# Transforms of a fused FFT and mixture-of-experts kernel: each scatter of 128 token rows waits for a PSUM copy of its own

## The chip, the cores and the metric

The kernel runs on one core of one Trainium2 chip. The metric is the time of the whole program in device microseconds (us), and lower is better. Names of engines are those of the profile: PE is the matrix engine, DVE the vector engine, ACT the scalar engine, POOL is GpSimd, SP the queue that issues most DMAs. L164 means line 164 of the kernel before.

## What is computed

The input x has 8 batches of 3072 rows with 256 values each, in fp32. The program computes the real part of a 2-D Fourier transform of each batch, sends every resulting row (a token, 24576 in all) to one of 8 experts, and runs a second network over all tokens:

```python
X = np.fft.fft(np.fft.fft(x, axis=1), axis=2).real          # 8 x 3072 x 256
x = X.reshape(24576, 256)
e = argmax of the cosine of x with the 8 expert rows; gate = its softmax probability
x = gate * (np.maximum(x @ w1[e], 0) @ w2[e])                # per token, its own expert
out = ((x @ w_a) * (x @ w_b)) @ w_out
```

## The kernel before, in words

The program has three stages one after the other. The **transforms** (span up to about 558 us) take the 8 batches in turn. The **experts** follow (up to about 1790 us), and then the second network. Only the transforms are touched.

The work of a batch b has two halves.

- `s1(b, s)`, 8 steps. Each step has two groups (h = 0, 1) of four matmuls at L343 into one of two PSUM banks, and behind each group ACT copies the bank to `yt` (L347). A profile shows each of these fp32 matmuls as two records, so that a whole half has 128 of them.
- `s2(b, t)` with `s3(b, t - 2)`, 12 steps. A step multiplies `yt` into two PSUM tiles `psb` and `psa` (L360, 8 records), ACT copies `psb` to `zs` (L361), DVE makes `zc` (L363), and two steps later PE multiplies both into a third tile (L376, L379), which ACT copies to `qs` (L387) and DVE adds and subtracts into the token rows `xo` (L388, L390). There are two buffers for each of these PSUM tiles, and one `xo` buffer for even and one for odd batches, so the rows of batch b must have left `xo` before step t = 2 of batch b + 2 writes there.

When the rows of a batch are complete, `route` (DVE, a generator that goes on by a few instructions at each step) computes for each row its place `posi` among the rows of its expert. `spread` (L164) then sends 128 rows of `xo` to these places in DRAM (the tensor `xs`) by an indirect DMA that POOL issues: the **scatter**. A batch has 24 of them, the transforms issue 168, and the rest of the 192 for `xs` fall in the first expert groups. POOL also computes two of the four `fold_v` pieces of the next batch's input (L244).

The order on each engine is written out by hand: work that has no step of its own is appended to lists (`act_q`, `dve_q`, `pool_q`) and taken off by `drain(queue, n)` at fixed places. Before the change `pool_q` holds both the folds and the scatters. It is drained by 2 in each step of s1 and by 3 in each step of s2. As `route` of batch b - 1 delivers its 24 places about four steps into s2 of batch b, POOL gets them in a row there, and issues them one behind the other: a burst. A scatter waits for the scatter eight before it and for its rows, for nothing else.

At the end of the transforms what is left of the 168 is issued. The expert stage begins with group 0; for group 1 POOL multiplies rows by their gates (`weigh`, L737, L738) and computes a low part (`halves`, L755), and the weight splits on ACT and DVE (L727, L728) write memory that the even `xo` buffer held, so they wait for its scatters to land.

Of the kernel before, what the change touches and what calls it, by code (L numbers as in the profile page):

```python
# [34 lines left out]
NROWS = E * REGION + GT  # L35
# [102 lines left out]
def moe_kernel(ctx, tc, x, emb, tau, w1, w2, wa, wb, wo, pa, pt, pr, nat, out):  # L138
    nc = tc.nc
    ve, sc, gp, pe, sy = nc.vector, nc.scalar, nc.gpsimd, nc.tensor, nc.sync  # L140
    dep = mybir.DependencyInfo(mybir.DependencyClass.Sync, mybir.DependencyReason.DATA)

    dram = ctx.enter_context(tc.tile_pool(name="dram", bufs=1, space=DRAM))
    xs = dram.tile([NROWS, ROW], F32, name="xs")
# [16 lines left out]
    scatters = []  # L161

    def spread(idx_ap, src, dst, last, key):
        i = gp.indirect_dma_start(  # L164
            out=dst[:, :],
            out_offset=bass.IndirectOffsetOnAxis(ap=idx_ap, axis=0),
            in_=src,
            in_offset=None,
            bounds_check=last,
            oob_is_err=False,  # L170
        ).ins
        tc.declare_no_dep(i, group=key, reason="rows of different tokens")
        tc.add_to_no_dep_group(key, i)
        return i


    p1 = ExitStack()
    p1b = ExitStack()
# [33 lines left out]
    def bank():  # L212
        uses[0] += 1
        return banks[uses[0] % 2][:, 0:384]
# [8 lines left out]
    def load_x(n):  # L223
        b, c = divmod(n, 4)
        if b == B:
            return
        t = xr_p.tile([96, 8, D], F32, name="xr")
        sy.dma_start(t, x[b].rearrange("(p n) d -> p n d", p=96)[:, 8 * c:8 * c + 8, :])
        xr[b, c] = t

    def pair(b, c):
        if (b, c) not in xf:
            xf[b, c] = big[(4 * b + c) % 6][0:96, :].rearrange("p (n d) -> p n d", n=8)
        return xr[b, c], xf[b, c]

    def fold_u(b, c, h):
        a, f = pair(b, c)
        n = slice(4 * h, 4 * h + 4)
        ve.tensor_tensor(f[:, n, 1:128], a[:, n, 1:128], a[:, n, 255:128:-1], ALU.add)

    def fold_v(b, c, eng, h):
        a, f = pair(b, c)
        n = slice(4 * h, 4 * h + 4) if h is not None else slice(0, 8)
        eng.tensor_tensor(f[:, n, 129:256], a[:, n, 1:128], a[:, n, 255:128:-1], ALU.subtract)  # L244

    def fold_e(b, c):
        a, f = xr.pop((b, c)), xf[b, c]
        sc.copy(f[:, :, 0:256:128], a[:, :, 0:256:128])
# [86 lines left out]
    def s1(b, s):  # L335
        f = xf[b, s // 2]
        state["step"] += 1
        if s == 0:
            yts[b] = [yt_p.tile([128, NQ, 128], F32, name=f"yt{h}") for h in range(2)]
        for h in range(2):  # L340
            ps = bank()
            for n in range(4):
                pe.matmul(ps[:, 96 * n:96 * n + 96], lhsT=f[:, 4 * (s % 2) + n, 128 * h:128 * h + 128],  # L343
                          rhs=f1[0:96, :], start=True, stop=True)
            dst = yts[b][h][:, :, 16 * s:16 * s + 16].rearrange("p q (n c) -> p q n c", c=4)
            src = ps.rearrange("p (n q c) -> p q n c", n=4, c=4)
            sc.copy(dst, src)  # L347
            if b:
                drain(act_q, 1)

    def s2(b, t):
        state["step"] += 1
        ya, yb = yts[b]
        za = z_p.tile([128, 2, 137], F32, name="zc")
        zb = z_p.tile([128, 2, 137], F32, name="zs")
        pb = psb.tile([128, 2, 138], F32, name="psb")
        pa_ = psa.tile([128, 512], F32, name="psa")[:, 0:274].rearrange("p (i m) -> p i m", i=2)
        for p, y, r in ((pb, yb, rhb), (pa_, ya, rha))[::1 if t else -1]:
            for i in range(2):
                pe.matmul(p[:, i, :], lhsT=y[:, 2 * t + i, :], rhs=r, start=True, stop=True)  # L360
        sc.copy(zb, pb[:, :, 0:137])  # L361
        for i in range(2):
            ve.scalar_tensor_tensor(za[:, i, :], sgnx, pb[:, i, 137:138], pa_[:, i, :], ALU.mult, ALU.add)  # L363
            advance()
        zt[b, t] = (za, zb)
# [41 lines left out]
        if t1 == NT:  # L407
            act_q.append(lambda: square(b, 1, 11))

    act_q, dve_q, pool_q, routes = [], [], [], []  # L410

    def drain(q, n):
        for _ in range(min(n, len(q))):
            q.pop(0)()

    def folds(b):
        for c in range(4):
            dve_q.append(lambda c=c: fold_u(b, c, 0))
            dve_q.append(lambda c=c: fold_u(b, c, 1))
            if c < 2:  # L420
                pool_q.append(lambda c=c: fold_v(b, c, gp, None))
            else:
                dve_q.append(lambda c=c: fold_v(b, c, ve, 0))
                dve_q.append(lambda c=c: fold_v(b, c, ve, 1))

            def rest(c=c):
                fold_e(b, c)
                load_x(4 * b + c + 3)

            dve_q.append(lambda c=c, rest=rest: act_q.insert(0, rest))  # L430

    seg = {}
    for n in sorted({2 * (t1 - t0) for c in CHUNKS.values() for t0, t1 in c} | {2 * NT}):
        s = c1.tile([128, E, n], F32, name=f"seg{n}")
# [15 lines left out]
    def route(b, t0, t1, turn):  # L450
# [16 lines left out]
        for q in range(2):  # L467
            yq = y[:, q, :].rearrange("p (t one) -> p t one", one=1)
            for i, n_ in enumerate((3, 3, 2)):
                c = MAIN + LGC[i]  # L470
# [68 lines left out]
        for i in range(h):  # L539
            for q in range(2):  # L540
                pool_q.append(lambda a=posi[:, q * h + i:q * h + i + 1], r=xo[b][:, NT * q + t0 + i, 0:ROW]:
                              scatters.append(spread(a, r, xs, NROWS - 1, "xs")))
        yield
        if b == HB - 1 and t1 == NT:
            yield from table1(new)
# [3 lines left out]
    def advance(n=1):  # L549
        for _ in range(n):  # L550
            if routes:
                for g in list(routes):
                    r = next(g, 0)
                    if r == 0:
                        routes.remove(g)
                    if r != 1:
                        break

    def start_route(b, t0, t1):
        routes.append(route(b, t0, t1, state["next"]))  # L560
        state["next"] += 1
# [361 lines left out]
    def first(c):  # L923
        for h in range(2):
            fold_u(0, c, h)
        fold_v(0, c, gp if c != 2 else ve, None)

    for b in range(B):
        last = b == B - 1
        if not last:  # L930
            folds(b + 1)
        for s in range(8):
            if b == 0 and s < 6:
                if s == 0:
                    routes.append(embed())
                if s % 2 == 0:
                    first(s // 2 + 1)
                else:
                    fold_e(0, s // 2 + 1)
                    load_x(s // 2 + 4)  # L940
            s1(b, s)
            drain(pool_q, 2 if b or s > 5 else 0)
            if b == 0:
                advance(7)
                drain(dve_q, s > 3)
                continue
            if s == 0:
                s3(b - 1, 10)
                s3(b - 1, 11)
                post(b - 1, 9, 12)  # L950
                act_q.append(lambda b=b - 1, c=CHUNKS.get(b - 1, ((0, NT),))[-1]: start_route(b, *c))
            if last:
                drain(act_q, s < 3)
                advance(8)
                if s == 0:
                    assert "tab1" in half
                    load_w(0)
                if s == 4:
                    load_w(1)
                if s in (4, 5):  # L960
                    split_w(0, s - 4)
            elif s < 3:
                drain(dve_q, 3 if s else 2)
                drain(act_q, s)
            else:
                advance(7)
        if b == 0:
            while routes:
                advance()
            su.close()  # L970
        chunks = {t1 + 1: (t0, t1) for t0, t1 in CHUNKS.get(b, ())}
        if last:
            for g in range(2):
                load_g(g)
        for t in range(NT + (2 if last else 0)):
            if t < NT:
                s2(b, t)
            if t >= 2:
                s3(b, t - 2)
            if t in (5, 8, 11):  # L980
                post(b, t - 5, t - 2)
            if t == NT + 1:
                break
            if t - 1 in chunks:
                act_q.append(lambda b=b, c=chunks[t - 1]: start_route(b, *c))
            if t % 3:
                drain(dve_q, 1)
            drain(act_q, 2)
            drain(pool_q, 3)
            if last:  # L990
                advance(1)
                if t == 6:
                    weigh(0)
                if t == 8:
                    turn(0)
        drain(dve_q, 20)
    drain(pool_q, (B - 1) * 2 * NT - len(scatters))
    assert len(scatters) >= (B - 1) * 2 * NT
    p1b.close()
# [294 lines left out]
```

## Time and profile before

| | before |
|---|---|
| median of 3 runs | 4059.99 us (4057.02 to 4069.61) |
| profiled execution, its own time | 4083.66 us |
| profiled execution, span | 4081.7 us |
| busy share of the span: PE, PE weight loads, DVE, ACT, POOL | 95%, 86%, 76%, 42%, 28% |
| mean granted TensorE clock | 0.956 of full speed |

The span runs from the first to the last instruction. The profile page shows the whole program; the change concerns only the first seventh of it, so its shares say little here. The slices of the page, tables of busy time by stretch, and instructions in order of time within one batch are what to read.

### The profile page before, as it was taken

The page shows a single profiled execution, that of the slowest core. Times are in us where ns is not written, and L with a number is a line of the kernel's source. Part 1 is how long each engine was busy: PE and PEld are TensorE (multiplying, and loading weights), DVE is VectorE, ACT ScalarE, POOL GpSimd, SP SyncE. Part 2 cuts the span into 40 slices and gives each one's busy share as a digit, 9 for nine tenths or more (in the row PEclk, how much of TensorE's full clock was granted, in tenths as well). Part 3 has the DMA queues.
Part 4 walks back from the last instruction along what each step waited for, and adds up shares of the span by engine and source line. Part 5 has one row for each costly group of instructions (what it writes and reads, how often), then busy time and mean ns, then how long its engine had stood idle before and what let it go on. Part 6 is the DMA issues. An engine that isn't in the chain of part 4 may idle for free.

```text
span 4081.7 us, 67996 instructions
## 1 busy us (share of the span) xinstructions
PE 3859.6 (95%) x25556; PEld 3515.0 (86%) x25556; DVE 3084.0 (76%) x5097; ACT 1698.2 (42%) x3025; POOL 1123.4 (28%) x1017
## 2 busy tenths in 40 slices
PE   8675789999999999999999999999999999999998
PEld 8574789999999999988888888888888888888887
DVE  6343378888888888777877778787877778777876
ACT  4233355666666666643333333333333333333332
POOL 2425245666666665300000000011000000000001
PEclk8577589999999999999999999999999999999999
DMA  5223225533233323133334334444433333443331
GB/s 146 86 84 104 90 65 161 179 117 111 77 108 113 117 75 98 48 122 135 137 136 148 138 139 138 138 144 144 138 136 137 135 138 137 149 138 138 138 128 66
DMA packets 255046, 497.83 MB, mean 122 GB/s; under 512 B 151540, under 2 KB 184060, under 8 KB 245884
## 3 DMA queue, kind: packets, MB, share of 16 engines
q1 hardware_dynamic: 236284, 442.04, 33.4%
q0 software_dynamic: 18432, 51.44, 3.5%
q8 instruction: 201, 3.29, 0.3%
q14 instruction: 129, 1.06, 0.1%
HBM read 568.14 MB, written 95.14 MB: 163 GB/s over the span
## 4 chain that ended last, share of the span: by engine, by line
issue 56%; PE 22%; POOL 9%; DVE 6%; another core or an unknown queue 3%; ACT 2%; DMA 1%; SPq 0%; POOLq 0%; ACTq 0%; DVEq 0%
PE ps L343 4%; POOL out_dram L164 4%; PE psh L772 3%; PE psh L773 2%; PE psh L771 2%; DVE s L728 2%; POOL xl L755 2%; PE psy L793 2%; PE psy L794 2%; PE psy L795 2%; PE psb L360 1%; PE psa L360 1%; ACT s L727 1%; PE ps L376 1%
## 5 line engine op out<-in xcount | busy, mean ns | idle before, releaser
L164 POOL DMA_INDIRECT out_dram<-o,ig x192 | 214.1, 1115 | 2095.1 <-ACT o L1189 2043.6
L1185 PE MATMUL po<-wo,gl 128*128 128x256 f32 x2304 | 652.0, 283 | 19.2 <-DVE gl L1167 19.2
L1162 ACT CAST gh<-big 128x512 fp32r<-128x512 f32 x576 | 358.0, 621 | 743.6 <-DVE big L1156 743.6
L1183 PE MATMUL po<-wo,gh 128*128 128x256 f32 x2304 | 647.9, 281 | 0.5 <-ACT gh L1162 0.5
L1184 PE MATMUL po<-wo,gh 128*128 128x256 f32 x2304 | 645.7, 280 | 0.0
L1115 PE MATMUL pp<-xo,slab 128*128 128x512 f32 x1440 | 580.3, 403 | 8.2 <-DVE big L1141 6.8
L728 DVE TENSOR_TENSOR s<-big,s 128x1024 fp32r<-128x1024 f32 x412 | 535.4, 1300 | 55.0 <-ACT s L727 54.3
L1117 PE MATMUL pp<-xo,slab 128*128 128x512 f32 x1440 | 569.7, 396 | 0.0
L1116 PE MATMUL pp<-xo,slab 128*128 128x512 f32 x1440 | 566.6, 393 | 0.0
L1184 PEld LDWEIGHTS po<-wo,gh 128*128 128x128 f32 x2304 | 434.1, 188 | 89.9
L1183 PEld LDWEIGHTS po<-wo,gh 128*128 128x128 f32 x2304 | 432.5, 188 | 88.5 <-ACT gh L1162 0.9
L772 PE MATMUL psh<-xl,s 128*128 128x256 f32 x1648 | 471.6, 286 | 20.6 <-POOL xl L755 17.8
L793 PE MATMUL psy<-hh,s 128*128 128x256 f32 x1648 | 466.9, 283 | 0.0
L794 PE MATMUL psy<-hl,s 128*128 128x256 f32 x1648 | 466.4, 283 | 0.0
L795 PE MATMUL psy<-hh,s 128*128 128x256 f32 x1648 | 465.9, 283 | 0.0
L771 PE MATMUL psh<-xh,s 128*128 128x256 f32 x1648 | 464.5, 282 | 1.4 <-ACT xh L754 1.4
L773 PE MATMUL psh<-xh,s 128*128 128x256 f32 x1648 | 464.7, 282 | 0.0
L1185 PEld LDWEIGHTS po<-wo,gl 128*128 128x128 f32 x2304 | 433.5, 188 | 24.3 <-DVE gl L1167 24.3
L1133 ACT COPY big<-pp 128x512 f32<-128x512 f32 x288 | 169.2, 588 | 662.3 <-PE pp L1117 585.5
L776 ACT ACTIVATE hh<-psh 128x512 fp32r<-128x512 f32 x412 | 246.8, 599 | 442.2 <-PE psh L773 438.3
L727 ACT CAST s<-big 128x1024 fp32r<-128x1024 f32 x412 | 428.6, 1040 | 0.0
L1167 DVE TENSOR_TENSOR gl<-big,gh 128x512 fp32r<-128x512 f32 x576 | 392.4, 681 | 0.3
(198 smaller groups left out, 8518.1 us busy)
## 6 DMA issues: line engine op xcount, KB each, us to landing
slab<-slabs SPq DMA_DIRECT2D x282, 896.0 KB
big<-in_w_dram SPq DMA_DIRECT2D x206, 1024.0 KB
big<-xs SPq DMA_DIRECT2D x103, 264.0 KB
ytd<-big SPq DMA_DIRECT2D x103, 256.0 KB
xr<-in_x_dram SPq DMA_DIRECT2D x32, 768.0 KB
big<-ytd SPq DMA_DIRECT2D x24, 1024.0 KB
slabs<-slab SPq DMA_DIRECT2D x12, 896.0 KB
xs<-xo,posi POOLq DMA_INDIRECT x192
```

Of the source, the lines that this page charges most:

```text
L728: ve.tensor_tensor(lo, r, hi.bitcast(F32), ALU.subtract)
L772: pe.matmul(ps[:, i, :], lhsT=wh, rhs=lo[:, k, :], start=False, stop=False)
L773: pe.matmul(ps[:, i, :], lhsT=wl, rhs=hi[:, k, :], start=False, stop=(k == 1))
L793: pe.matmul(ps[:, c, :], lhsT=wh, rhs=a[:, i, :], start=st, stop=False, skip_group_check=True)
L794: pe.matmul(ps[:, c, :], lhsT=wh, rhs=l[:, i, :], start=False, stop=False, skip_group_check=True)
L795: pe.matmul(ps[:, c, :], lhsT=wl, rhs=a[:, i, :], start=False, stop=(f == 7), skip_group_check=True)
L1115: pe.matmul(ps, lhsT=t[:, wh, :], rhs=xh, start=start, stop=False, skip_group_check=True)
L1116: pe.matmul(ps, lhsT=t[:, wh, :], rhs=xl, start=False, stop=False, skip_group_check=True)
L1117: pe.matmul(ps, lhsT=t[:, wl, :], rhs=xh, start=False, stop=True, skip_group_check=True)
L1183: pe.matmul(ps, lhsT=ht, rhs=wos[0][:, f, :], start=(first_ and r % 2 == 0), stop=False, skip_group_check=True)
L1184: pe.matmul(ps, lhsT=ht, rhs=wos[1][:, f, :], start=False, stop=False, skip_group_check=True)
L1185: pe.matmul(ps, lhsT=lt, rhs=wos[0][:, f, :], start=False, stop=last_, skip_group_check=True)
```

## The change

The folds get a list of their own, `fold_q`, from which one is taken after each step of s1. The scatters stay in `pool_q`, but the fixed drains are gone. In their place `mark(i)` is called behind a PSUM copy i on ACT: it notes the copy and drains one scatter (two while more than 24 are queued), and the first scatter drained gets a dependency on that copy, so POOL waits for it. Marks are the two `yt` copies of each step of s1 (from batch 2 on) and the `zs` copy of each step of s2 (from batch 1 on). What is still queued at the end is drained without marks.

```diff
+    marks = []
+
+    def mark(i):
+
+        marks[:] = [i.ins]
+        drain(pool_q, 2 if len(pool_q) > 24 else 1)
+
+    def scatter(idx_ap, src):
+        i = spread(idx_ap, src, xs, NROWS - 1, "xs")
+        if marks:
+            tc.add_manual_dep(i, marks.pop().name, dep, reason="rows one by one")
+        scatters.append(i)
...
-            sc.copy(dst, src)
+            i = sc.copy(dst, src)
+            if b > 1:
+                mark(i)
+            elif b:
+                marks[:] = [i.ins]
...
-        sc.copy(zb, pb[:, :, 0:137])
+        i = sc.copy(zb, pb[:, :, 0:137])
+        if b:
+            mark(i)
...
-                pool_q.append(lambda c=c: fold_v(b, c, gp, None))
+                fold_q.append(lambda c=c: fold_v(b, c, gp, None))
...
-                              scatters.append(spread(a, r, xs, NROWS - 1, "xs")))
+                              scatter(a, r))
...
-            drain(pool_q, 2 if b or s > 5 else 0)
+            if b or s > 5:
+                drain(fold_q, 1)
...
-            drain(pool_q, 3)
...
+    marks.clear()
     drain(pool_q, (B - 1) * 2 * NT - len(scatters))
```

No arithmetic is added or taken away. The instructions of PE, DVE, ACT and SP stand in the same order as before (line numbers shift by 13 to 19); on POOL they move. Three places matter.

The first is POOL in the transforms, from the scatters of batch 0 on (`xr` is the loaded input, `big` the folded one). Before:

```order
L164 DMA xs<-xo,posi 198912x267 x24
L244 TENSOR_TENSOR big_69<-xr 96x8x127
L244 TENSOR_TENSOR big_70<-xr 96x8x127
L164 DMA xs<-xo,posi 198912x267 x24
L244 TENSOR_TENSOR big_73<-xr 96x8x127
L244 TENSOR_TENSOR big_74<-xr 96x8x127
```

and with the change:

```order
L164 DMA xs<-xo,posi 198912x267 x9
L257 TENSOR_TENSOR big_69<-xr 96x8x127
L164 DMA xs<-xo,posi 198912x267 x2
L257 TENSOR_TENSOR big_70<-xr 96x8x127
L164 DMA xs<-xo,posi 198912x267 x22
L257 TENSOR_TENSOR big_73<-xr 96x8x127
L164 DMA xs<-xo,posi 198912x267 x2
L257 TENSOR_TENSOR big_74<-xr 96x8x127
```

The 24 scatters in a row become 7 in the last steps of s2 and, in the next batch, 2 in step 0 of s1, a fold, 2 in step 1, a fold, 12 in the other steps of s1 and 1 at step t = 0 of s2.

The second place is the waits of these scatters (DMASW is an earlier scatter's landing, Activation an ACT instruction, DVE the new places `posi`). Before, at the start of a batch's scatters:

```order
L164 DMA xs<-xo,posi 198912x267 [waits DMASW0_49,DVE_49,Activation_49]
L164 DMA xs<-xo,posi 198912x267 [waits DMASW1_49]
L164 DMA xs<-xo,posi 198912x267 [waits DMASW2_49]
L164 DMA xs<-xo,posi 198912x267 [waits DMASW3_49]
L164 DMA xs<-xo,posi 198912x267 [waits DMASW4_49]
```

and with the change:

```order
L164 DMA xs<-xo,posi 198912x267 [waits DMASW0_49,DVE_49,Activation_49]
L164 DMA xs<-xo,posi 198912x267 [waits DMASW1_49,Activation_49]
L164 DMA xs<-xo,posi 198912x267 [waits DMASW2_49,Activation_49]
L164 DMA xs<-xo,posi 198912x267 [waits DMASW3_49,Activation_49]
L164 DMA xs<-xo,posi 198912x267 [waits DMASW4_49,Activation_49]
```

Each now waits for an ACT copy as well.

The third place is POOL where the transforms end and the experts begin. Before:

```order
L164 DMA xs<-xo,posi 198912x267 x45
L738 COPY big_69<-big_69 32x8
L164 DMA xs<-xo,posi 198912x267 x3
L737 TENSOR_TENSOR big_70<-big_69 128x512
L738 COPY big_69<-big_69 32x8
L755 TENSOR_TENSOR xl<-big_70,xh 128x512
```

and with the change:

```order
L164 DMA xs<-xo,posi 198912x267 x43
L757 COPY big_69<-big_69 32x8
L164 DMA xs<-xo,posi 198912x267 x18
L756 TENSOR_TENSOR big_70<-big_69 128x512
L757 COPY big_69<-big_69 32x8
L774 TENSOR_TENSOR xl<-big_70,xh 128x512
```

Of the 18 scatters there, 5 have a copy to wait for and 13 are the rest that is drained without marks; before, 3 stood there.

## Rows read from the trace of the kernel before

**Rows 1.** The profile page: busy tenths in 40 slices, PE and its clock.

```profile
PE   8675789999999999999999999999999999999998
...
PEclk8577589999999999999999999999999999999999
```

**Rows 2.** Busy time by stretch of the transforms (stretch, its length, engines, clock).

```profile
core 0: us, PE busy (x) PEld busy (x) DVE busy (x) ACT busy (x) POOL busy (x), PEclk, DMA share, GB/s
41.20:61.50 20.30, 20.00 (x172) 16.81 (x172) 14.10 (x45) 11.67 (x41) 2.50 (x1) 0.95 0.31 80
62.00:78.30 16.30, 16.17 (x151) 15.70 (x150) 12.83 (x35) 13.16 (x41) 2.75 (x1) 1.00 0.70 187
62.00:108.40 46.40, 38.01 (x329) 33.78 (x328) 30.11 (x98) 23.66 (x76) 17.76 (x16) 0.92 0.43 125
108.40:558.40 450.00, 311.03 (x1998) 279.83 (x1997) 175.62 (x677) 157.31 (x502) 175.56 (x166) 0.66 0.29 90
267.10:297.30 30.20, 30.20 (x150) 29.67 (x150) 11.33 (x43) 13.86 (x42) 0.00 (x0) 0.50 0.31 79
```

**Rows 3.** Instructions in order of time, one burst (batch 2, 163 to 198 us).

```profile
start us, us, engine line op out<-in xcount [idle before <-releaser]
...
163.41 0.99 POOL L164 DMA_INDIRECT xs<-xo,posi  x1 [38.84 <-ACT zs L361]
...
164.71 0.97 POOL L164 DMA_INDIRECT xs<-xo,posi  x1 [0.30 <-issue]
...
171.77 0.43 PE L379 MATMUL ps<-zc,tpq 128*64 128x137 f32 x4
...
184.00 0.28 ACT L387 COPY qs<-ps 128x137 f32<-128x137 f32 x1 [11.63 <-remote]
...
184.97 0.72 PE L376 MATMUL ps<-zs,tpq 128*64 128x137 f32 x4 [7.02 <-DVE xo L390]
...
193.93 4.67 POOL L244 TENSOR_TENSOR big<-xr 96x1016 f32<-96x1016 f32 x2
...
197.44 0.28 ACT L387 COPY qs<-ps 128x137 f32<-128x137 f32 x1 [3.92 <-remote]
```

**Rows 4.** Waits, 80 to 640 us: total us, times, longest.

```profile
POOL xs L164 <- ACT zs L361: 152.8, 5, 43.2
ACT qs L387 <- remote: 86.2, 9, 13.7
```

**Rows 5.** Groups of POOL instructions, 62 to 558.4 us: busy us, mean ns.

```profile
L164 POOL DMA_INDIRECT xs<-xo,posi x168 | 165.9, 988 | 294.0 <-ACT zs L361 152.8 <-ACT qs L387 42.8 <-issue 42.3
...
L244 POOL TENSOR_TENSOR big<-xr 96x1016 f32<-96x1016 f32 x11 | 26.0, 2394 | 11.0 <-DMA xr<-in_x_dram 11.0
```

**Rows 6.** Instructions in order of time, end of the first burst (118 to 125 us).

```profile
118.93 0.98 POOL L164 DMA_INDIRECT xs<-xo,posi  x1 [0.30 <-issue]
...
120.96 0.32 PE L343 MATMUL ps<-f,big 96*128 96x96 f32 x1 [1.77 <-issue]
...
123.11 0.28 ACT L387 COPY qs<-ps 128x137 f32<-128x137 f32 x1 [10.84 <-remote]
```

**Rows 7.** The same, start of the first burst (89 to 95 us).

```profile
89.11 1.13 POOL L164 DMA_INDIRECT xs<-xo,posi  x1 [20.08 <-DVE zc L363]
...
89.86 0.40 PE L379 MATMUL ps<-zc,tpq 128*64 128x137 f32 x4
...
90.37 0.28 ACT L387 COPY qs<-ps 128x137 f32<-128x137 f32 x1 [0.37 <-PE ps L379]
...
93.36 0.28 ACT L387 COPY qs<-ps 128x137 f32<-128x137 f32 x1 [1.49 <-PE psa L360]
```

**Rows 8.** The same, 12 scatters that begin inside s1 of batch 7 (511 to 532 us).

```profile
513.01 0.97 POOL L164 DMA_INDIRECT xs<-xo,posi  x1 [29.66 <-ACT yt L347]
...
520.74 0.48 ACT L347 COPY yt<-ps 128x384 f32<-128x384 f32 x1 [1.23 <-PE ps L343]
...
530.70 0.39 ACT L361 COPY zs<-psb 128x274 f32<-128x274 f32 x1 [3.92 <-PE psb L360]
```

**Rows 9.** POOL in order of time where the experts begin (505 to 580 us).

```profile
554.40 1.04 POOL L737 TENSOR_TENSOR big<-big 128x512 f32<-128x512 f32 x1
...
567.38 2.00 POOL L755 TENSOR_TENSOR xl<-big,xh 128x512 fp32r<-128x512 f32 x1 [11.23 <-ACT xh L754]
```

More of the change, by code (lines that the diff above doesn't have):

```diff
@@ L408, in post @@
             act_q.append(lambda: square(b, 1, 11))
-    act_q, dve_q, pool_q, routes = [], [], [], []
+    act_q, dve_q, pool_q, fold_q, routes = [], [], [], [], []
     def drain(q, n):
```

## The prediction

> **What bounds the kernel now.** I began with the slices of the page [rows 1]. From the seventh slice on PE is busy at nine tenths and its clock is full; before that PE is at five to eight tenths and the clock moves between whole and half. So the transforms, and they alone, have room. The table by stretch [rows 2] says how much. The half s2 of batch 0, beside which no scatter runs, takes 20.3 us with PE busy for 20.0 of them; the half s1 of batch 1 takes 16.3 at full clock, and s1 of batch 4, at clock 0.50, takes 30.2 with PE busy throughout. A batch that nothing holds up would thus take 16.3 + 20.3 = 36.6 us. Batch 1 takes 46.4, and batches 2 to 7 together 450.0, which is 75.0 each, with PE busy for 311 of the 450.
>
> The instructions in order of time show where the rest goes [rows 3]. POOL issues its 24 scatters from 163.41 on, one each 1.28 us (0.98 of work and 0.30 between), until the fold at 193.93. PE's matmuls that begin at 171.77 last 0.43 us, but the ACT copy that reads them starts only at 184.00, after 11.63 us of idle time whose releaser is unknown ("remote"); PE, which waits for what comes of this copy, idles 7.02 us. The next copy of this kind comes at 197.44, behind the end of the burst. The table of waits puts 86.2 us on `qs` from this cause alone [rows 4]. It isn't the copies alone: in the tail of the first burst single s1 matmuls start with 1.77 us of idle time that no wait explains [rows 6]. I read this as PE being held from telling others that it is done, and in the end from going on, while scatters follow each other closely. The copy of 123.11 starts 3.2 us behind the end of the last scatter's issue (118.93 + 0.98) [rows 6]. At the start of a burst the copies are still on time (matmuls at 89.86 of 0.40 us, copy at 90.37, with a scatter issued at 89.11), and at 93.36 the copy is 1.49 us idle [rows 7]. So a first scatter costs nothing, and after a few at 1.28 us the hold has built up.
>
> **The change, part by part.** *Taken from s2:* the burst of 24. In its place 7 scatters stand at the last steps, one per step, and a step lasts 20.3 / 12 = 1.7 us when nothing holds it; one is left for step 0. Each waits for that step's `zs` copy, so that if PE falls behind, the scatters do too. No row shows a row of scatters at 1.7 us in s2. The bounds are nothing (the first scatters of a burst [rows 7]) and, from above, what a burst costs, 3.2 us per scatter [rows 6], 7 x 3.2 = 22 us. I take 3 us per batch, near the lower bound, since the hold feeds back on the next scatter, which it did not before.
>
> *Put into s1:* 16 scatters and two folds. POOL needs 16 x 1.28 = 20.5 and 2 x 2.39 = 4.8 us for them [rows 3, 5], 25.3 together, against 16.3 us of PE at full clock. POOL therefore falls behind its marks, copies that are waited for are long done, and scatters follow at 1.28 us. One place shows this beside s1: from 513.01 on six scatters run at this distance, and the ACT copy of 520.74 still starts with PE as its releaser and no long wait; behind the border to s2, at 530.70, the copy is late by 3.92 [rows 8]. That s1 ran at half clock. So s1 at half clock (30.2 us) bears the scatters, and at full clock it either waits for POOL (25.3) or is held. I take 28 us, between the two; the ends are 16.3 and, if the hold comes back as in a burst, 25.3 + 3.2 + 16.3 / 2 = 37.
>
> *The order of buffers:* the last scatter of batch b now stands at step 0 of s2 of batch b + 2, and DVE writes the same `xo` at step 2. With landing 3.2 us after the issue it can be late by a few us if POOL is behind. It is not added twice: it lies inside the 28 and the 3.
>
> *The folds* come at the same steps as before and are needed a batch later; the wait of 11.0 us that one had for its input [rows 5] stays hidden for the same reason. The extra waits themselves cost nothing on POOL, where only scatters and folds are queued behind; ACT, DVE and SP get no wait. In fact the scatters had 152.8 us of waiting for `zs` copies as it was [rows 4].
>
> A batch then takes 28 + 20.3 + 3 = 51.3 us, and six of them 308 in place of 450: 142 us less. Batch 1 has no scatters in s1: 16.3 + 23.3 = 39.6 in place of 46.4: 7 less.
>
> *At the end* 13 scatters without a mark stand ahead of POOL's work for group 1: 13 x 1.28 = 16.6 us, and the weight splits on ACT and DVE wait until they have landed, 3.2 us more. Before, `weigh` started at 554.40 and the low part `xl` at 567.38 [rows 9], just in time for PE. I put 18 us on this, once, out of 0 (group 0 covers it) to 16.6 + 3.2 + 5 = 25 with a slow clock behind it.
>
> The sum is -142 - 7 + 18 = -131 us. The profiled execution, 4083.7 us by its own time, would come to 4083.7 - 131 = 3953; it stands 23.7 us above the median of the three runs. Against the median I forecast 4060 - 131 = **3929 us**.
>
> **The rivals.**
>
> *Free running.* The spacing ends the hold altogether and s1 takes only POOL's 25.3 us or less. With 25.3 + 20.3 = 45.6 a batch a batch 29.4 less, the sum is 6 x -29.4 = -176, -10 for batch 1 (46.4 - 36.6) and 18 at the end, -168, and the time 3892; with the full 36.6 a batch it is -230 - 10 + 18 = -222 and 3838. For it speaks the first scatter of a burst [rows 7], against it POOL's 25.3 us in s1. For the whole case about 3865.
>
> *The burst has only moved.* The order says that each scatter waits, but a copy that is done holds nothing back. If in s1 at full clock the hold sets in as it does in s2, and s2 loses 6 us, twice my 3, a batch takes 37 + 20.3 + 6 = 63.3 us, six of them 380, batch 1 42.6, and the sum is -70 - 4 + 18 = -56: 4004 us. The copy of 530.70 [rows 8] speaks for it, that of 520.74 against it.
>
> *A lock per scatter.* If what is lost is lost for each scatter, wherever it stands, spreading gives nothing: 24 x 0.98 = 23.5 us a batch before and after, and the time is 4060 us where group 0 covers the end. The Trainium skill has such a rule ("SBUF — State Buffer", section "Who interferes with whom"): GpSimd and DVE share a port pair that one holds for a whole instruction, and "PE and ACT never wait on anyone". Here the scatters keep 0.98 us throughout the burst and it is PE's results that come late [rows 3], so the trace does not bear this out.
>
> *Slower: each scatter a round trip.* A scatter now waits for a copy, and the copy for PE. If one scatter alone held PE's messages until it had landed, 0.98 + 3.2 = 4.2 us, scatters and steps would take turns: s1 16 x 4.2 = 67.2, s2 8 x 4.2 + 4 x 1.7 = 40.4, so 107.6 us a batch in place of 75. That is 32.6 x 6 = 196, 8 in batch 1 (16.3 + 7 x 4.2 + 5 x 1.7 = 54.2 in place of 46.4) and 18 at the end, 222 more and 4282 us. It decides from (75 - 4 x 1.7) / 24 = 2.8 us per scatter on. The late copies of the bursts speak for it; the copy of 90.37 [rows 7] and the six scatters of batch 7 [rows 8] speak against it.
>
> **How the numbers follow.** The forecast gets 0.52, free running 0.20, the moved burst 0.15, the lock 0.05, slower 0.08. A measurement of this kernel can tell about 0.3% (12 us) from no change. The first three are faster by more than that, 0.87; the lock is the same, 0.05; the last is slower, 0.08. The range leaves out the lock, the slower case and a little of the tails: it goes from the lower end of the free case, 3838, to the moved burst with 16 us more, 4020, which is 2.7 us a batch.
>
> **What would show it.** In the profile after, POOL's scatters stand 1.3 us or more apart and are spread over s1 and the end of s2; the "remote" waits of ACT on `qs` fall from 86.2 us [rows 4] to under 25; batches 2 to 7 take 45 to 57 us each; the experts begin near 420 us, and the first slices of the page have a higher clock. At the start of the experts there is one hole of 10 to 25 us in PE. The mechanism is wrong if late copies go on at the same total though no 24 scatters stand in a row, or if they stay away and the batches still take 70 us. My size for s1 is wrong if s1 takes 17 us or 37.

## The result, and the profile after

| | before | after |
|---|---|---|
| median, 4 runs each | 4061.84 us (4057.02 to 4069.61) | 3951.56 us (3947.09 to 3956.46) |
| ratio, 95% interval | | 0.9727 (0.9707 to 0.9747) |
| profiled execution, span | 4081.7 us | 3948.6 us |
| mean granted TensorE clock | 0.956 | 0.980 |
| last matmul of the transforms | 554.4 us | 401.6 us |

The change made this pair 110 us faster, against the 131 us of the forecast. The second half of this section tells where these 110 us are, and the experiments then show that they aren't there everywhere: in three of the six measurements behind this document, on three chips, the kernel before has nothing to gain from the change.

The slices of the changed kernel's page, in the same rows as [rows 1]: in place of six slices at five to eight tenths there are four at eight tenths (a slice is 98.7 us), and the clock is at 0.8 or more everywhere.

```profile
PE   9888899999999999999999999999999999999998
...
PEclk8888899999999999999999999999999999999999
```

The table by stretch answers to [rows 2]; columns as there. The stretches are batch 1, s1 and s2 of batch 2, the batches 2 to 7, and the border to the experts.

```profile
62.00:99.00 37.00, 36.23 (x330) 32.19 (x326) 31.59 (x105) 24.82 (x81) 8.95 (x8) 1.00 0.46 125
99.00:115.80 16.80, 16.50 (x151) 15.88 (x150) 12.82 (x31) 13.02 (x41) 13.56 (x11) 1.00 0.71 201
115.60:149.60 34.00, 24.56 (x176) 20.54 (x177) 18.72 (x69) 11.20 (x38) 15.59 (x16) 0.75 0.29 93
99.00:401.60 302.60, 251.45 (x1974) 222.20 (x1974) 193.00 (x651) 149.64 (x482) 173.38 (x159) 0.85 0.43 131
401.60:424.00 22.40, 12.67 (x88) 10.93 (x88) 7.38 (x26) 6.75 (x18) 16.02 (x17) 0.81 0.33 110
```

Batches 2 to 7 take 302.6 us in place of 450.0, 50.4 each. Of these 147.4 us, 87.8 are idle time of PE (139.0 before, 51.2 after), and 59.6 are busy time of PE (311.0 and 251.5), whose granted clock went from 0.66 [rows 2] to 0.85 of full speed. But s1 is free (16.8 us) and s2 is not (34.0 us, PE busy for 24.6 of them, at clock 0.75). The batches 3 to 6 are the same, s1 16.6 to 18.1 us and s2 32.0 to 33.7; in batch 7 it is 26.4 and 21.5. Instructions in order of time, batch 2, show why:

```profile
114.26 0.98 POOL L164 DMA_INDIRECT xs<-xo,posi  x1 [0.30 <-issue]
...
115.11 0.48 ACT L360 COPY yt<-ps 128x384 f32<-128x384 f32 x1 [0.58 <-PE ps L356]
...
119.38 0.97 POOL L164 DMA_INDIRECT xs<-xo,posi  x1 [0.30 <-issue]
120.14 0.48 ACT L360 COPY yt<-ps 128x384 f32<-128x384 f32 x1 [4.55 <-remote]
...
120.67 2.21 PE L377 MATMUL psb<-rhb,yt 128*128 128x138 f32 x8 [4.30 <-issue]
...
127.11 0.97 POOL L164 DMA_INDIRECT xs<-xo,posi  x1 [0.30 <-issue]
...
130.21 0.39 ACT L378 COPY zs<-psb 128x274 f32<-128x274 f32 x1 [2.51 <-remote]
...
139.52 0.97 POOL L164 DMA_INDIRECT xs<-xo,posi  x1 [11.43 <-ACT zs L378]
```

POOL is behind its marks from the folds on. So 13 scatters stand in a row again, nearly all 1.28 us apart, from 111.41 to 127.11, across the border from s1 to s2. The first copies beside them are on time (115.11), then come the late ones (120.14, 4.55 us, "remote"; 130.21). From 139.52 on most scatters follow an ACT copy, and in this half there is no "remote" wait any more. In the table of waits, over all transforms after 62 us, the remote waits that remain are these:

```profile
ACT zs L378 <- remote: 25.8, 7, 5.3
...
DVE zc L382 <- remote: 23.1, 5, 5.3
...
ACT yt L360 <- remote: 15.4, 5, 4.6
```

Before, beside the 86.2 us on `qs` [rows 4], there were these:

```profile
ACT zs L361 <- remote: 32.2, 9, 8.0
...
DVE zc L363 <- remote: 11.9, 2, 9.8
```

So the total fell from 130.3 us to 64.3: none is left on `qs`, and half of the whole remains, most of it beside the rows of 13 or just behind them.

What "remote" stands for can be made out from the records of semaphore updates that the trace keeps, though no view prints them. PE's instructions count up one semaphore (102). The copy of 184.00 [rows 3] starts 0.02 us behind an update of it that is recorded at 183.98, while the matmuls that the copy reads had ended at 172.20. All 16 remote waits of ACT and DVE over 1 us in the transforms of before, and all 17 of the changed kernel, end 0.02 to 0.10 us behind such an update. It is thus PE's own update that comes late.

The rest of the account: from the last matmul of the transforms to a fixed matmul a quarter through the experts it is 314.0 us before and 331.4 after, 17.4 more. -152.8 + 17.4 and 2.3 in the later stages make the -133.1 between the two spans.

### The profile page after: what moved, and what is told of

It is laid out like the page before. It is cut to its first block, busy times and chain, and to the rows that moved or that the text cites. A ratio compares the mean times of both kernels' runs of the same rounds, so it can differ in the third digit from the quotient of the medians.

```text
span 3948.6 us, 68109 instructions
## 1 busy us (share of the span) xinstructions
PE 3807.7 (96%) x25556; PEld 3463.4 (88%) x25556; DVE 3104.2 (79%) x5097; ACT 1695.7 (43%) x3025; POOL 1128.4 (29%) x1017
## 4 chain that ended last, share of the span: by engine, by line
issue 58%; PE 20%; POOL 9%; DVE 7%; ACT 2%; DMA 1%; another core or an unknown queue 1%; SPq 0%; POOLq 0%; ACTq 0%; DVEq 0%
POOL out_dram L164 4%; PE psh L791 3%; PE psh L792 3%; PE psh L790 2%; POOL xl L774 2%; DVE s L747 2%; PE psy L812 2%; PE psy L813 2%; PE psy L814 2%; PE ps L356 2%; PE psb L377 1%; PE psa L377 1%; ACT s L746 1%; PE ps L395 1%; POOL tq L869 1%
```

## The experiments

All call the kernel before "before" and have runs of it beside them on the same chip. These runs fell into two kinds, and this is the main finding: medians of 4078.84 (chip 14) and 4057.07 (chip 15), as in the pair above, and 3904.13 (chip 1), 3903.98 (chip 5) and 3903.55 (chip 8). I call the first kind *late* chips, the second *prompt* ones. The names say more than is shown: each of the five chips was measured on one occasion, so what belongs to a chip and what to its state at that moment can't be told apart.

### Before, again (prompt chip)

No edit.

> The kernel before, unchanged, profiled a second time. The profiled execution of before stood 23.7 us above the median of its runs. If that was this execution's own longer holds, the second profile comes out near 4060 us, batches 2 to 7 take about 71 us each in place of 75.0, and the experts and the second network take the same as in the first (within 3 us). If a profile as such costs these 24 us, it is 4080 us or more again, with 75 us a batch.

Measured: 3902.88 us. Both expectations missed. Each batch takes some 44 us, there is no remote wait in the transforms, and the rows show a whole row of scatters beside prompt copies (columns as in [rows 3]):

```profile
119.30 0.67 DVE L244 TENSOR_TENSOR big<-xr 96x508 f32<-96x508 f32 x1
119.37 1.45 POOL L164 DMA_INDIRECT xs<-xo,posi  x1 [0.30 <-issue]
...
119.75 0.40 PE L379 MATMUL ps<-zc,tpq 128*64 128x137 f32 x4
119.90 0.35 DVE L363 SCALAR_TENSOR_TENSOR zc<-sgnx,psb,psa 128x137 f32<-128x137 f32 x1
...
120.20 0.28 ACT L387 COPY qs<-ps 128x137 f32<-128x137 f32 x1 [1.18 <-PE ps L379]
...
120.53 5.00 DVE L516 TENSOR_SCALAR mx<-mx 128x24 f32<-128x24 f32 x1
...
120.82 4.67 POOL L244 TENSOR_TENSOR big<-xr 96x1016 f32<-96x1016 f32 x2
...
126.17 0.73 PE L376 MATMUL ps<-zs,tpq 128*64 128x137 f32 x4 [3.13 <-DVE xo L390]
```

The scatter of 119.37 is the last of 24 at 1.28 us, and the copy of 120.20 follows its matmuls (119.75, 0.40 us) at once; PE's update is recorded at 120.18. What this kernel still loses here, 6 to 8 us in each s2, is another thing: a DVE instruction on 128x24 elements lasts 5.00 us, to the end of POOL's two folds. In every batch from 2 to 6 one DVE instruction beside the two folds, not always this one, is as long (5.00, 5.72, 5.56, 5.56, 5.12 us).

### No wait (prompt chip)

```diff
-        if marks:
-            tc.add_manual_dep(i, marks.pop().name, dep, reason="rows one by one")
```

> The changed kernel, with its new order on POOL, but no scatter waits for a copy. Theory (distance): without the waits POOL issues what stands in its queue one behind the other as soon as the places are known, rows of 24 come back, and with them the late copies: 4040 us (4010 to 4070), s2 40 us or more per batch. Rival (the folds' own list and the places in the program do it): about 3952, as the changed kernel.

Measured: 3901.0 us beside 3904.13, ratio 0.9993 (0.9983 to 1.0003). Both times that were expected were for a late chip. On a prompt chip the order on POOL alone changes nothing; the run says nothing of the late ones.

### A pause behind each scatter of before (prompt chip)

```diff
+    def paced(a, r):
+        scatters.append(spread(a, r, xs, NROWS - 1, "xs"))
+        gp.memset(gap, 0.0)
...
-                              scatters.append(spread(a, r, xs, NROWS - 1, "xs")))
+                              paced(a, r))
```

> The kernel before, with a POOL memset of 128x256 behind each scatter of the transforms, so that scatters stand some 1.8 to 2.0 us apart and still wait for no copy. Theory (distance alone): the copies are on time, the remote waits on qs fall from 86 us to under 20, and POOL itself, 24 x 1.9 + 4.8 = 50 us a batch, is the longest: about 50 to 55 us a batch and 3930 us (3890 to 3990). Rival (waiting for a copy is what counts, since then no message of PE is under way beside a scatter): copies are late for the whole row as before, and the row is longer, 24 x 1.9 = 46 us in place of 31: 4100 us or more.

Measured: 3924.86 us beside 3904.13, ratio 1.0051 (1.0035 to 1.0068). The memset, of 128x256, took only 0.33 us and made the distance 1.46 us. The time lies in the range of the theory, but bears nothing out: no message was late without the pause either. With none to cure, the longer row costs 0.5%.

### A row of scatters that move nothing (prompt chip)

```diff
+        if b == 0:
+            for _ in range(24):
+                pool_q.append(lambda: spread(far, padt[:, 0, :], xs, NROWS - 1, "xs"))
```

> The kernel before, and 24 more scatters in s2 of batch 0, where none stood; all their indices lie beyond the last row, so that they move no row. Theory (what POOL issues holds PE's messages): s2 of batch 0 takes 40 to 48 us in place of 20.3, as s2 of batches 2 to 7 does. Rival (the rows on their way, 128 x 1068 bytes a scatter, hold them): s2 of batch 0 stays under 23 us.

Measured: 3913.42 us, and s2 of batch 0 took 20.9 us. No remote wait stands in its transforms; the 9 us over 3904 are in s1 of batch 1, 24.7 us at clock 0.70. On a prompt chip no row of scatters makes a message late, so this doesn't tell the theories apart; it was done again below.

### The changed kernel, again (prompt chip)

No edit.

> The changed kernel, unchanged, beside fresh runs of the kernel before. In the last experiments the kernel before itself took 3904 us, 156 us less than in the pair of the prediction, and no copy of its transforms waited for a late message of PE, though its bursts of 24 scatters stood there with the same 1.28 us between. Theory (the late messages belong to the chip or its state at the time, and the change is worth only what they cost): where the kernel before takes about 3904 us, the changed one takes 3890 to 3925 us, within 0.5%; where before takes about 4060 us, the changed one is again 100 to 120 us faster. Rival (the change saves its 110 us wherever it runs): 3795 us beside 3904.

Measured: 3924.19 us beside 3903.98, ratio 1.0054 (1.0040 to 1.0067): here the change is 0.5% slower. The rival falls. What it costs stands in the waits of DVE, 62 to 377 us, and in the same place of a batch:

```profile
DVE xo L407 <- DMA xs<-xo,posi: 47.0, 6, 8.9
```

```profile
174.20 0.97 POOL L164 DMA_INDIRECT xs<-xo,posi  x1 [0.30 <-issue]
...
176.77 0.30 DVE L407 TENSOR_TENSOR xo<-ps,qs 128x137 f32<-128x137 f32 x1 [8.75 <-DMA xs<-xo,posi]
...
177.51 0.72 PE L395 MATMUL ps<-zs,tpq 128*64 128x137 f32 x4 [7.15 <-DVE xo L409]
```

The last scatter of the rows of two batches before is issued 12 us into s2 (of batch 3 in these rows), and the first write of the new rows into the same `xo` waits for its landing: 47.0 us in six waits. The changed kernel's s2 takes 30.2 us in batch 2, against 26.7 in the second profile of before. Over the batches 2 to 7 that makes 277.7 us in place of 262.3.

### Folds of before on DVE (late chip)

```diff
-            if c < 2:
-                pool_q.append(lambda c=c: fold_v(b, c, gp, None))
-            else:
-                dve_q.append(lambda c=c: fold_v(b, c, ve, 0))
-                dve_q.append(lambda c=c: fold_v(b, c, ve, 1))
+            dve_q.append(lambda c=c: fold_v(b, c, ve, 0))
+            dve_q.append(lambda c=c: fold_v(b, c, ve, 1))
...
```

(The drains of `dve_q` take one more in s1, and come in three of four steps of s2 in place of two of three.)

> The kernel before with all four fold_v pieces of a batch on DVE, none on POOL; scatters as before. In the second profile of before, where no copy was late, each s2 of batches 2 to 6 still lost 6 to 8 us against the free 20.2 us, and in batch 2 a DVE instruction on 128x24 elements lasted 5.00 us while POOL's two folds ran (4.67 us). Theory (a fold on POOL holds DVE): without them s2 takes 20 to 22 us, six batches lose 6 us less each, and the time is about 3868 us beside 3904 (3860 to 3885). Rival (DVE has no room for the folds, or the loss has another cause): 3895 us or more. Where before takes about 4060 us, the late messages stay and it takes 4020 to 4060.

Measured: 4062.77 us beside 4078.84, ratio 0.9961 (0.9940 to 0.9982). The late messages stay (78.1 us of remote waits on `qs`), as expected of a late chip, and the time is 3 us over the range given for one. Whether the folds' 5 us can be had on a prompt chip by this edit alone was not measured.

### Folds of the changed kernel on DVE (late chip)

The same edit, on the changed kernel.

> The changed kernel with all fold_v pieces on DVE. In its second profile DVE waited 47.0 us (6 waits, 8.9 at most) with its first write into xo for the scatters of two batches before to land, since POOL ends its 16 scatters and two folds of s1 only some 14 us into s2. Theory (buffer order): POOL ends 2 x 2.39 + 0.4 = 5.2 us earlier, the wait shrinks from 7.8 to about 2.6 us a batch, and the time falls by 6 x 5.2 = 31 us to about 3893 us beside 3924. Rival (the wait is for something else, or DVE is now the bound): 3915 us or more. Where before takes about 4060 us: 30 to 50 us less than the 3952 of the changed kernel.

Measured: 3935.94 us beside 4078.84, ratio 0.9646 (0.9619 to 0.9674). The wait for landings is gone (one of 1.5 us), s2 takes 21 to 22 us. But the row of scatters now begins earlier and holds s1: 22 to 25 us, 32.6 us of remote waits on `yt`. 16 us less than the changed kernel's 3952 on another chip, where 30 to 50 were expected: without the folds between, 16 scatters in s1 are one row.

### An even spread (late chips, twice)

On top of the last one:

```diff
-            if b > 1:
+            if b > 1 and (h or s % 2):
                 mark(i)
...
-                advance(7)
+                advance(12)
```

> As the run before, and the scatters spread over the whole batch: route goes on by 12 in place of 7 in s1 from step 3 on, so that the places are known when s2 begins, and in s1 only three of four copies are marked; 11 or 12 scatters in s2 and 12 in s1, the last one a step before s2 ends its first step. Theory: neither the buffer order nor a row of scatters holds anything, a batch takes 37 to 39 us, and the time is 3904 - 6 x 6.5 = 3865 us (3850 to 3885), under both kernels; also where before takes about 4060 us, then under 3900. Rival (DVE, with the folds and the faster route, becomes the bound): s1 takes 19 us or more and the time is 3895 or more.

> The even version (folds on DVE, faster route, three of four s1 copies marked) once more, beside before on whatever chip this is. Where before takes about 4070 us: 3915 us again. Where it takes 3904 us and no message is late: theory, a batch takes 37 to 38 us and the time is 3860 us (3850 to 3880), so that this version is faster than both kernels on both kinds of chip; rival (the wait on a copy costs there what it cost the changed kernel, or DVE is the bound): 3895 us or more.

Measured: 3915.26 us beside 4078.84, ratio 0.9595 (0.9567 to 0.9622), 15 us over what was expected; once more on chip 15, 3918.25 beside 4057.07, 0.9656 (0.9640 to 0.9672). A batch takes 43.4 us, not 37 to 39. In s2 scatters follow the `zs` copies some 1.75 us apart and s2 takes 20.6 to 21.6 us, as free as [rows 2] have it. In s1 rows at 1.28 us are left and hold PE:

```profile
118.21 0.98 POOL L164 DMA_INDIRECT xs<-xo,posi  x1 [0.30 <-issue]
119.49 0.97 POOL L164 DMA_INDIRECT xs<-xo,posi  x1 [0.30 <-issue]
...
120.57 3.73 PE L356 MATMUL ps<-f,big 96*128 96x96 f32 x16 [1.77 <-issue]
...
134.50 0.97 POOL L164 DMA_INDIRECT xs<-xo,posi  x1 [0.78 <-ACT zs L378]
```

### Three tests in one (late chip)

```diff
-        if marks:
+        if marks and b not in (2, 3, 4, 5):
...
+        if b in (4, 5):
+            gp.memset(gap, 0.0)
...
+        if b == 0:
+            for _ in range(24):
+                spread(far, padt[:, 0, :], xs, NROWS - 1, "xs")
```

(The memset is 128x512; the last lines stand ahead of the steps of s2.)

> The changed kernel with three tests in one profile: (a) 24 scatters that move no row (all indices beyond the last row) in s2 of batch 0; (b) no waits for the scatters of the rows of batches 2 and 3; (c) no waits but a POOL memset of 128x512 behind each scatter of batches 4 and 5 (some 1.7 us from one to the next). It says something only where before takes about 4060 to 4080 us; where it takes 3904, all three leave PE's messages on time and only the buffer order shows. Theory (issue at a distance of 1.28 us holds PE's messages, whatever released it): (a) s2 of batch 0 takes 40 us or more in place of 20.3; (b) the batches 3 and 4, in which those scatters run, take 65 to 75 us, batch 2 about 51; (c) batches 5 and 6 take 45 to 55 us. Rival 1 (the rows under way hold them): (a) under 23 us. Rival 2 (the order on POOL and the folds' own list did it, not the waits): (b) 51 us as batch 2. Rival 3 (only a wait for a copy helps, distance does not): (c) 65 us or more.

Measured: 4008.67 us beside 4057.07, one execution. This is the run that decides, and each part of it rests on one or two batches. By stretch: (a) s2 of batch 0; batch 2, its scatters with waits; (b) batches 3 and 4, without; (c) batch 6, with pauses:

```profile
41.00:82.50 41.50, 26.65 (x172) 22.32 (x172) 15.61 (x45) 11.50 (x41) 19.22 (x19) 0.65 0.17 40
119.90:171.80 51.90, 41.41 (x331) 36.35 (x328) 32.70 (x101) 24.95 (x82) 29.45 (x26) 0.87 0.43 125
171.80:232.10 60.30, 44.49 (x330) 38.62 (x328) 33.30 (x103) 25.02 (x82) 40.09 (x35) 0.80 0.41 121
232.10:302.10 70.00, 51.01 (x330) 46.61 (x328) 28.66 (x102) 25.49 (x81) 28.57 (x26) 0.68 0.31 93
358.70:410.90 52.20, 39.37 (x333) 34.40 (x331) 32.56 (x103) 25.11 (x81) 42.33 (x52) 0.87 0.42 134
```

(a) 24 scatters that move no row, begun some 8 us ahead of it, double s2 of batch 0, 41.5 us in place of the 20.3 of both kernels without them, and the rows of that stretch show the same signs as a burst:

```profile
59.36 0.63 DVE L384 SCALAR_TENSOR_TENSOR zc<-sgnx,psb,psa 128x137 f32<-128x137 f32 x2 [8.65 <-remote]
59.54 0.97 POOL L164 DMA_INDIRECT xs<-padt,far  x1 [0.30 <-issue]
...
62.09 0.97 POOL L164 DMA_INDIRECT xs<-padt,far  x1 [0.30 <-issue]
...
66.34 0.28 ACT L408 COPY qs<-ps 128x137 f32<-128x137 f32 x1 [10.90 <-remote]
```

So the rows under way aren't needed, and rival 1 falls. What is left is the issue on POOL and the small packets that come with it: each of these scatters still sends 48 packets, as many as one that moves rows, but 17 of them carry 0.01 MB together. (b) With the order of the changed kernel but no wait, the two batches take 60.3 and 70.0 us, batch 2 with waits 51.9. The same two batches took 65.7 and 77.7 in the first profile of before, on another chip, so the order alone may be worth 5 to 8 us each; the larger part needs the waits, and rival 2, which asked for 51 us, falls. (c) With a pause and no wait the scatters stand 1.68 us apart:

```profile
385.27 0.98 POOL L164 DMA_INDIRECT xs<-xo,posi  x1 [0.17 <-issue]
386.22 0.57 POOL L189 MEMSET gap<- 128x512 f32 x1
386.96 0.97 POOL L164 DMA_INDIRECT xs<-xo,posi  x1 [0.17 <-issue]
...
394.57 0.30 DVE L409 TENSOR_TENSOR xo<-ps,qs 128x137 f32<-128x137 f32 x1 [12.32 <-DMA xs<-xo,posi]
```

From 345 us, where the paced scatters begin, to the end of the transforms no engine has one remote wait. (Batch 5 tells nothing: the last scatters of batch 3, without a pause, still run in its s1.) The 52.2 us of batch 6 are mostly the order of the buffer again (12.32 us for landings), since POOL, paused, is later still. So distance suffices in this run, without any wait for a copy, and rival 3 falls: 0.40 us more between scatters kept every message on time.

### Even, and even with a pause (prompt chip)

```diff
+        if b < B - 2:
+            gp.memset(gap, 0.0)
```

(Behind each scatter of the even version, 128x256.)

> The even version with a POOL memset of 128x256 behind each scatter of batches 0 to 5, which in the run with pauses took 0.33 us and set scatters 1.46 us apart. In the even version the rows at 1.28 us inside s1 still hold PE: 9.4 us of remote waits and s1 of 20 to 21 us in place of 16.4 (batches 2 to 5). Theory: at 1.46 us, as at 1.68 us in the mixed test, no message is late, s1 takes 17 to 18 us, a batch 39 to 40 in place of 43, and the time is 4 x 3.5 = 14 us under the even version on a chip where before takes about 4070 us, the same within 5 us where before takes 3904. Rival (1.46 us is still too near): remote waits of 8 us or more and the same time as the even version.

> The even version beside its variant with pauses, on the same chip. Where before takes about 4070 us: 3915 to 3920 us, as twice before. Where before takes 3904 us: theory, 3860 us (3850 to 3880), since neither the buffer order nor a fold on POOL is in the way; rival, 3895 or more.

Measured, on chip 8: with the pause 3901.3 us, 0.9996 (0.9987 to 1.0006); without, 3899.89 beside 3903.55, 0.9991 (0.9982 to 1.0001). The two are the same there, as expected of a prompt chip; the distance of 1.46 us was not tried on a late one. The 3860 us were missed. Halves are free (s1 16.4, s2 20.4 to 21.6 us), but between them PE stands still for about 4 us: the faster route puts its matmul ahead of s2, before DVE has made its operand. The row, and the waits of PE from 62 to 354 us:

```profile
123.48 0.36 PE L527 MATMUL ps<-inc,prt 128*128 128x8 f32 x2 [3.42 <-DVE inc L511]
```

```profile
PE ps L527 <- DVE inc L511: 17.3, 5, 3.6
```

The even version is thus the best of those run: 3.4 to 4.1% under before on late chips (the changed kernel 2.7% in its own pair), and equal to before on a prompt one; on another prompt one the changed kernel is 0.5% slower. It never ran beside the changed kernel on one chip.

## Why the prediction was right, and where not

**The mechanism** was right for this pair. The bursts held PE's messages, in the rows at 1.28 us and not at the last steps of s2, and the remote waits fell from 130.3 us to 64.3. The mixed test showed the three parts of it that the prediction only read from rows: issue holds, even where no row moves; distance releases; and a wait for a copy is one way to make distance. The two neighbours of the forecast were each right in one half of a batch: s1 ran free, and the burst had moved, 13 scatters in place of 24, across the next border. The rival of a lock per scatter falls with this, since the pauses leave all 24 in place; the rival of a round trip, 107.6 us a batch, falls with 50.4.

**A batch**, forecast 28 + 20.3 + 3 = 51.3 us, took 50.4, but by two errors that cancel, which is luck. s1 was put at 28 us and took 16.8, which by the prediction's own sign makes its size for s1 wrong: the two folds keep scatters apart until the row of 13 begins at 111.41, and by then s1 is nearly done. s2 was put at 23.3 and took 34.0: the same row, "POOL therefore falls behind its marks", lies there, since POOL's 25.3 us of work don't go into the 16.3 us of PE: the last of the row ends at 128.08, 12.5 us behind the border of 115.6. The prediction saw the backlog and charged it to the wrong half. Its 3.2 us per scatter [rows 6] is the lag of one copy behind a whole burst, not the price of a scatter, and as the time to a landing it is too long (2.6 us from issue, the median of 120 scatters in the second profile of before). A backlog that a stage builds up is paid in the next one.

**Batch 1**, forecast 39.6, took 37.0: the 3 us for seven spaced scatters in s2 were nothing. **The order of buffers** was "not added twice", that is, priced at nothing of its own. On the late chip it is hidden (DVE's first write into `xo` comes at 133.60, after 0.72 us of waiting for `qs`), because PE is held just as long; on a prompt chip the same order makes DVE wait 47.0 us, and the changed kernel is 20 us slower than before there. It is what is late next, and it should have been a term with its own bound. Set chip against chip, which is a reading across occasions, before takes 158 us more on a late chip than on a prompt one (4061.84, 3903.98) and the changed kernel 27 more (3951.56, 3924.19): some 131 us of holds are gone, and 20 come back by what the change itself costs.

**The end**, forecast 18, measured 17.4, but not for the reason given. On a prompt chip the kernel before, which has no row of 13 scatters there, needs 325.0 us for the same stretch in which it needs 314.0 on the late one, with a PE wait of 6.0 us for ACT's `hh`; the changed kernel needs 332.2 there, with a wait of 11.4 (7.4 in the pair). So about 7 us belong to the change, and about 11 appear where the transforms end early, whatever stands on POOL; why was not traced. The size was luck.

**The sum**, -131 us, met the profiles, -133.1. The median moved by 110. The step that failed is carrying the gain of one profiled execution to the median: that execution stood 23.7 us above its median, and I subtracted its whole gain from the median as if these 23.7 us lay outside the transforms. The changed kernel doesn't have them: its profiled execution (3950.49 us) is at its median. So they most likely were holds, and went with them. No second profile of before on a late chip was taken to show it.

**What the prediction could not know** is that the holds are there on some chips, or at some times, and not on others. Nothing in one profile tells that; on chips 1, 5 and 8 the whole cause is missing, and on chip 5 the change loses 0.5%. On a prompt chip another hold shows: beside POOL's folds a DVE instruction lasts 5.00 us, to the end of the second fold, while beside a scatter DVE's `big` of 119.30 takes 0.67 us (0.61 at 126.16, with POOL idle). The Trainium skill's rule from the third rival ("SBUF — State Buffer", section "Who interferes with whom"), of a port pair that GpSimd and DVE share and that one holds for a whole instruction, has its place there. The trace agrees with it for the folds, though the DVE instruction lasted through two of them, and shows no such hold beside a scatter.

What stays open: why chips or occasions differ, and by what path an issue on POOL makes PE's update late. Whether the recording of the runs takes part isn't shown. Whether the no-wait order or the 1.46 us distance cures a late chip as a whole was not measured either.

## What to carry to other kernels

Where an engine's results come late though its instructions are short and nothing is queued, look at who else issues in that time, and put distance between those issues before moving any work. Work that is spread must fit, with all that its engine does besides, into the stretch it is spread over, or the rest of it stands in a row at the next border; and the buffer that it reads from comes free later. Before a gain of some per cent is believed, measure the old kernel on more than one chip, and at more than one time.

## What the runs showed of the hardware

- Indirect DMAs that POOL issues 1.28 us apart (0.98 us each) delayed PE's semaphore updates in some measurements and not in others: before takes 4057 to 4079 us on chips 14 and 15 and 3904 on chips 1, 5 and 8, each seen once. At 1.68 us there was no delay on chip 15, in one run. Scatters that write nothing delay too (41.5 us in place of 20.3).
- The traces of late chips also lack records. Of the updates of the eight semaphores on which scatters land, the first profile of before holds 139 to 520 each, that of chip 1 762 to 770; of PE's updates 3058 and 3150. The updates themselves arrive, or the kernel would stop; so the late chips seem to have trouble with this traffic as such, which is a reading and not shown. In all seven profiles from prompt chips no remote wait stands in the transforms.
- Two folds of POOL back to back hold one DVE instruction for 5.0 to 5.7 us on a chip without late messages.
